# Two transformer layers on one core: a queue order rewritten by a search, with the transfer queue left as it was

## The chip, the core and the metric

The kernel runs on one core of a Trainium2 chip. The core has five instruction queues that run side by side: TensorE (PE, the matrix multiplies; PEld is its weight load), VectorE (DVE), ScalarE (ACT), GpSimd (POOL) and SyncE (SP, which here issues transfers only). Each queue starts its instructions in the order in which they stand in it, and waits for other queues through semaphores. The metric is the device time of one execution in microseconds (us), lower is better; for the kernel before, the median of three runs is 456.8 us.

## What is computed

One attention layer and one MLP layer, applied twice with the same weights, over 2048 tokens of width 512, in bfloat16:

```python
x = A_x
x = x + _A_ref(_layernorm(x), A_wqkv, A_wo)                  # 32 heads of 16, causal, window of 256
x = x + _B_ref(_layernorm(x), B_w1, B_b1, B_w2, B_b2)        # 512 -> 1792, gelu (tanh form), -> 512
x = x + _A_ref(_layernorm(x), A_wqkv, A_wo)
x = x + _B_ref(_layernorm(x), B_w1, B_b1, B_w2, B_b2)

# inside _A_ref
scores = einsum("bhqd,bhkd->bhqk", q, k) * 16 ** -0.5
scores = where(0 <= i - j < 256, scores, -1e9)
p = softmax(scores);  o = einsum("bhqk,bhkd->bhqd", p, v);  return o @ wo
```

B_x is not used.

## The kernel before

**The work.** The tokens are cut into 16 tiles of 128, and the two repetitions make 32 tiles in a row, tau 0 to 31; all weights stay in SBUF. Attention goes by blocks b of two tiles (16 blocks over both repetitions), the MLP by ten jobs J of two or four tiles. Each operation is a node of a plan with a key, and the texts name operations by these keys:

- Layer norm of tile pair b: `bsN`, `baN` (DVE statistics, lines 584 and 586), `vpN` (add epsilon, line 590, on POOL or DVE), `pwN` (the power -0.5, line 596, on POOL), `xnN` (DVE, line 606, subtract and scale). N is the tile in layer 0 (before attention) and 32 plus the tile in layer 1 (before the MLP). `txN` (SP, line 611) then transposes xn by a DMA into xnTA (layer 0) or xnTB (layer 1); for the first four and last two of them PE does it (`tpN`), and `teN` copies the result out.
- Projections of block b (PE, line 632): `qb_i`, `kb_i`, `vtau`. `qeb_i` and `vetau` copy them out of PSUM (on DVE, line 573, or ACT, line 575); `keb_i` (DVE, line 666) writes keys into KT with a parity mask. `vs` (SP, line 681) copies values to the other half of the partitions.
- Attention of block b, in up to ten visits g: `scb_g` (PE, line 733, scores into two pairs of PSUM banks), `exb_g_0` and `exb_g_1` (ACT, line 740, the exponential), `mkb_g_n` (line 761, multiplication with the 0/1 mask, on DVE or POOL). After half of the visits: `pvb_cp` (PE, line 783), `odb_cp` (DVE, line 792, transpose out of PSUM), `rcb_cp` (DVE, line 796), `nmb_cp` (line 800, DVE or POOL), `otb_cp` (DVE, line 806). Then `optau` (PE, line 632, output projection) and `rstau` (DVE, line 832, residual).
- MLP job J: `mJ_fc` (PE), then for the first six chunks `gbJ_fc` (DVE, line 855, bias) and `gaJ_f` (ACT, line 858, gelu), for the others `geJ_fc` (ACT, line 863, both). `xbtau` (POOL, line 871, x plus the second bias), `ytau` (PE), `yatau` (DVE, line 875, residual), and the store.

A suffix as in `op7.2` is the third part of a group of matmuls that can be queued apart. PSUM has eight banks; a group takes one, two or four of them and gives them back with the operation that reads it out, so a wait for a bank is a wait for an exponential, a copy or an `od`.

**What sets the order.** Building the plan numbers the nodes 0 to 3079 and says for each what it reads and writes. Three lists written out as numbers then decide everything else: `_ORDER` is a permutation of all nodes, from which each engine's queue takes its own nodes; `_ALT` names the nodes that run on their second engine (a copy on ACT instead of DVE, a mask or normalization on POOL instead of DVE, an epsilon on DVE instead of POOL); `_BANKS` gives the first PSUM bank of each group as it comes up. `_Plan.run` applies them:

```python
for i in _ALT:
    nodes[i]["eng"], nodes[i]["fn"] = nodes[i]["alts"][1]
...
for i in _ORDER:
    nd = nodes[i]
    assert nd["deps"] <= seen
```

`_Sched.op` then records each node on its engine in that order, works out from reads, writes and banks which counters of other engines it has to wait for, and lets each node add one to its own engine's counter (a transfer adds 16 to one of eight counters). So the n-th signal of an engine's counter in the trace is the n-th node of that engine's queue, and each node's end can be read from the trace by name.

Of the kernel before, what the change touches and what calls it, by code (L numbers as in the profile page):

```python
# [19 lines left out]
class _Sched:  # L20
# [147 lines left out]
    14, 17, 0, 22, 33, 4, 7, 34, 18, 37, 1, 19, 13, 36, 26, 3, 46, 15, 8, 27, 9, 35, 56, 16, 41, 20, 39, 57, 60, 28,  # L168
    58, 40, 61, 30, 38, 59, 24, 2, 64, 62, 106, 65, 63, 104, 21, 66, 10, 47, 49, 32, 67, 11, 25, 107, 105, 68, 108, 23,
    109, 69, 31, 54, 29, 5, 80, 70, 110, 81, 113, 71, 55, 111, 114, 112, 72, 115, 82, 42, 73, 6, 83, 150, 74, 116, 117,  # L170
    84, 126, 118, 127, 119, 128, 120, 129, 324, 194, 130, 85, 196, 97, 98, 99, 86, 195, 100, 48, 152, 366, 87, 101,
    368, 88, 75, 153, 90, 322, 103, 91, 76, 367, 151, 102, 77, 89, 78, 154, 12, 92, 79, 155, 198, 197, 131, 199, 93,
    156, 132, 94, 133, 157, 134, 200, 136, 135, 202, 137, 203, 138, 96, 139, 325, 323, 121, 158, 95, 326, 122, 204,
    140, 216, 327, 159, 201, 143, 217, 144, 205, 145, 146, 141, 519, 123, 218, 124, 328, 207, 147, 125, 329, 219, 212,
    208, 170, 213, 171, 172, 43, 330, 214, 370, 206, 173, 209, 148, 371, 174, 175, 210, 149, 160, 161, 162, 372, 331,
    176, 520, 163, 215, 177, 521, 374, 164, 373, 220, 44, 211, 376, 142, 165, 221, 178, 375, 45, 166, 167, 168, 180,
    522, 169, 222, 379, 223, 181, 380, 182, 230, 523, 224, 183, 524, 231, 381, 225, 179, 226, 369, 232, 233, 184, 227,
    384, 234, 378, 185, 228, 385, 332, 229, 333, 51, 383, 342, 187, 386, 52, 334, 235, 377, 343, 335, 50, 237, 344,
    337, 394, 388, 345, 396, 382, 338, 188, 238, 236, 387, 189, 239, 190, 395, 346, 339, 240, 389, 336, 191, 398, 243,
    641, 347, 400, 348, 349, 241, 340, 350, 390, 399, 242, 352, 359, 527, 244, 402, 391, 341, 392, 351, 353, 192, 403,  # L180
    354, 306, 355, 360, 356, 361, 404, 407, 639, 357, 362, 409, 363, 193, 248, 405, 249, 262, 528, 250, 263, 408, 412,
    264, 401, 252, 393, 253, 414, 245, 246, 254, 290, 255, 247, 256, 413, 427, 257, 563, 525, 410, 259, 565, 526, 260,
    278, 261, 279, 275, 564, 640, 416, 276, 411, 428, 53, 415, 272, 422, 287, 186, 397, 281, 282, 284, 365, 288, 285,
    277, 273, 423, 406, 280, 539, 289, 540, 566, 529, 251, 530, 541, 274, 531, 542, 283, 532, 543, 307, 265, 266, 267,
    258, 269, 270, 286, 308, 533, 309, 268, 310, 311, 271, 291, 312, 313, 417, 292, 418, 293, 314, 294, 315, 419, 567,
    642, 420, 295, 643, 568, 316, 317, 318, 421, 644, 319, 569, 320, 429, 647, 430, 321, 296, 648, 570, 571, 431, 297,
    573, 298, 299, 645, 424, 425, 434, 572, 646, 300, 576, 426, 301, 577, 302, 574, 303, 358, 304, 432, 544, 545, 578,
    305, 581, 546, 435, 433, 547, 583, 534, 436, 548, 535, 580, 549, 550, 582, 437, 536, 551, 552, 579, 537, 553, 591,
    538, 556, 592, 649, 584, 650, 557, 438, 558, 585, 593, 651, 439, 595, 575, 440, 559, 898, 596, 652, 594, 586, 441,
    560, 597, 653, 487, 654, 587, 599, 659, 598, 600, 660, 655, 588, 656, 661, 896, 601, 662, 604, 899, 589, 657, 605,  # L190
    456, 602, 658, 457, 442, 458, 443, 606, 452, 444, 445, 446, 663, 453, 609, 459, 610, 460, 454, 466, 603, 467, 608,
    449, 611, 897, 450, 447, 900, 478, 607, 451, 479, 469, 461, 470, 472, 590, 463, 503, 473, 664, 612, 481, 624, 471,
    482, 901, 468, 464, 665, 613, 462, 484, 485, 474, 666, 625, 480, 904, 475, 448, 902, 667, 905, 476, 483, 614, 486,
    465, 364, 477, 488, 455, 554, 615, 619, 620, 489, 903, 490, 491, 616, 683, 617, 492, 685, 493, 494, 495, 618, 496,
    684, 497, 561, 668, 498, 626, 627, 687, 628, 621, 688, 622, 499, 623, 500, 501, 689, 504, 631, 691, 505, 502, 692,
    506, 690, 507, 629, 508, 509, 693, 916, 632, 630, 696, 1018, 686, 510, 917, 697, 1019, 511, 1016, 918, 695, 512,
    694, 919, 698, 701, 513, 514, 703, 700, 676, 920, 515, 669, 516, 702, 670, 671, 517, 699, 906, 518, 711, 677, 704,
    712, 672, 678, 705, 679, 907, 673, 713, 706, 680, 675, 715, 707, 908, 716, 909, 717, 708, 719, 1017, 910, 709, 721,
    724, 1020, 710, 1021, 725, 633, 739, 1024, 718, 720, 740, 744, 726, 745, 722, 723, 729, 634, 911, 730, 912, 714,
    921, 731, 922, 727, 923, 732, 940, 913, 942, 733, 924, 728, 1022, 914, 941, 925, 1023, 734, 943, 915, 637, 635,  # L200
    1025, 944, 735, 945, 636, 736, 946, 948, 737, 562, 949, 738, 926, 746, 950, 741, 742, 555, 952, 743, 953, 674, 947,
    747, 955, 638, 748, 927, 928, 954, 832, 749, 958, 681, 751, 929, 682, 959, 750, 752, 933, 753, 754, 934, 960, 1036,
    757, 935, 951, 758, 1026, 961, 936, 755, 957, 937, 1037, 962, 756, 1027, 930, 956, 968, 1275, 1038, 969, 1039, 931,
    1028, 1040, 1029, 932, 963, 970, 1030, 971, 972, 964, 775, 973, 776, 777, 778, 781, 974, 779, 782, 976, 965, 783,
    978, 764, 1273, 966, 784, 785, 977, 981, 975, 765, 766, 982, 786, 979, 787, 788, 767, 983, 789, 768, 986, 987, 790,
    985, 770, 771, 1276, 772, 1274, 984, 980, 988, 773, 1060, 774, 1061, 989, 1064, 990, 1065, 991, 1066, 759, 1062,
    992, 760, 792, 761, 793, 762, 817, 993, 1068, 763, 797, 1070, 818, 1063, 794, 1277, 802, 967, 819, 1278, 1069, 798,
    795, 994, 827, 848, 799, 803, 807, 995, 804, 812, 805, 1071, 828, 808, 1067, 806, 829, 800, 1001, 791, 809, 813,
    820, 1002, 796, 830, 996, 1003, 831, 822, 814, 769, 1004, 997, 1005, 810, 998, 823, 821, 1072, 849, 850, 780, 824,
    833, 815, 834, 825, 801, 835, 836, 811, 851, 837, 838, 826, 852, 839, 816, 999, 853, 1000, 840, 841, 842, 843,  # L210
    1006, 1073, 1279, 844, 845, 1074, 1008, 854, 1280, 846, 855, 847, 856, 1075, 857, 1078, 880, 858, 1079, 859, 860,
    861, 862, 1080, 1031, 863, 1041, 1032, 1033, 1077, 1034, 1082, 1088, 1035, 1009, 865, 1081, 866, 1090, 1042, 1076,
    1043, 1007, 1281, 1044, 1395, 1089, 1083, 1282, 1045, 1091, 1092, 867, 1084, 1093, 881, 882, 864, 868, 869, 1094,
    883, 1085, 1096, 1086, 884, 1097, 870, 885, 871, 872, 1010, 873, 1098, 1011, 1101, 886, 874, 1102, 887, 1099, 1100,
    888, 875, 889, 1095, 1103, 876, 1393, 1106, 1087, 877, 1107, 878, 890, 1105, 891, 1104, 892, 1108, 879, 893, 1317,
    1014, 894, 1318, 1015, 1110, 1293, 1294, 1396, 1283, 1109, 1284, 1319, 1295, 895, 1285, 1286, 1296, 1287, 1321,
    1320, 1297, 1111, 1322, 1012, 1323, 1298, 1013, 1112, 1288, 1299, 1300, 1325, 939, 1301, 1113, 1326, 1046, 1302,
    1289, 1114, 938, 1047, 1290, 1327, 1291, 1048, 1049, 1394, 1324, 1115, 1121, 1050, 1122, 1330, 1292, 1123, 1328,
    1332, 1124, 1116, 1125, 1117, 1118, 1331, 1119, 1335, 1120, 1310, 1336, 1128, 1333, 1053, 1054, 1311, 1126, 1337,
    1345, 1129, 1127, 1055, 1334, 1056, 1130, 1346, 1312, 1131, 1313, 1329, 1057, 1132, 1349, 1347, 1134, 1133, 1339,  # L220
    1351, 1314, 1348, 1303, 1304, 1305, 1338, 1135, 1350, 1306, 1353, 1397, 1652, 1355, 1316, 1352, 1340, 1307, 1052,
    1354, 1398, 1308, 1358, 1341, 1315, 1356, 1360, 1163, 1164, 1147, 1165, 1401, 1166, 1359, 1363, 1167, 1148, 1309,
    1149, 1364, 1150, 1362, 1141, 1058, 1151, 1142, 1143, 1361, 1365, 1144, 1402, 1145, 1437, 1158, 1438, 1357, 1159,
    1342, 1160, 1399, 1161, 1367, 1439, 1400, 1441, 1366, 1152, 1343, 1153, 1443, 1440, 1368, 1051, 1344, 1442, 1059,
# [722 lines left out]
```

## Time and profile before

| | |
|---|---|
| three runs | 456.17, 456.8, 457.9 us; median 456.8 |
| profiled execution | 457.15 us, of which 455.3 us is the span from the first to the last instruction of the program; mean granted PE clock 0.996 |
| busy (share of the span) | PE 420.6 us (92%), ACT 385.0 (85%), DVE 352.7 (77%), PEld 230.2 (51%), POOL 193.4 (42%) |
| exponential, 128x1024 | 300 on ACT, 1041 ns each, 283.1 us in all |
| mask | 139 on DVE, 529 ns mean; 97 on POOL, 1089 ns mean |
| transfers | 47900 packets, 22.17 MB; 60 packets of 16384 bytes on queue 8, kind "instruction" |

Everything that is asked of a profile here is asked of that one execution, on its own clock, which starts at the first instruction. An instruction's duration as the trace shows it overlaps the next one's on DVE and ACT by about 0.1 us; where a text speaks of a service time, it is the time from the later of its start and the previous operation's signal to its own signal (512-wide mask: 0.335 us on DVE, 1.117 on POOL). PE's busy share counts overlapping, modelled matmul ends, so it says that PE is seldom without work, and not that it works at its peak; PE's losses are better seen from the distance between the signals of neighbouring operations.

### The profile page before, as it was taken

Reading aid. Unit: us, or ns where it says so; the run is one execution under the profiler, and the core shown is the slowest. Engines: PE = TensorE matmul, PEld = TensorE weight load, DVE = VectorE, ACT = ScalarE, POOL = GpSimd, SP = SyncE. Lnnn points to the kernel's source line nnn. Section 1 sums busy time; section 2 is a strip of 40 time slices with the busy share of each in tenths; the row PEclk is TensorE's granted clock in tenths of the full one; section 3 lists DMA queues with packets and bytes.
Section 4 is the critical chain, followed back from the end, with each engine's and each line's share of the span. In section 5 each row is a group of like instructions: output and inputs, shape, how many; then the busy total and the mean of one; then the engine's idle time right before and its main releaser. Section 6 shows DMA issues by size and latency. Waiting matters only on the chain.

```text
span 455.3 us, 16821 instructions
## 1 busy us (share of the span) xinstructions
PE 420.6 (92%) x7506; PEld 230.2 (51%) x7579; DVE 352.7 (77%) x655; ACT 385.0 (85%) x456; POOL 193.4 (42%) x217
## 2 busy tenths in 40 slices
PE   8998999985779997899999999999999999999997
PEld 4564646543344553445455454555554454444673
DVE  5999689886775778894799867977897598756862
ACT  2997968987889899789998998999888989899633
POOL 4164634237331247632472754274243443526130
PEclk9999999999899999999999999999999999999999
DMA  8695311201400211310012021010232003002110
GB/s 243 186 218 166 77 33 24 44 10 18 86 15 1 25 23 41 76 26 1 14 35 58 1 56 37 10 42 3 62 50 62 1 4 79 14 1 67 60 48 24
DMA packets 47972, 23.25 MB, mean 51 GB/s; under 512 B 33180, under 2 KB 47900, under 8 KB 47900
## 3 DMA queue, kind: packets, MB, share of 16 engines
q1 hardware_dynamic: 47900, 22.17, 21.0%
q8 instruction: 60, 0.98, 0.9%
q14 instruction: 12, 0.10, 0.1%
HBM read 8.00 MB, written 2.10 MB: 22 GB/s over the span
## 4 chain that ended last, share of the span: by engine, by line
PE 69%; DVE 15%; ACT 12%; issue 3%; DMA 2%; POOL 0%; SPq 0%
PE ps L632 52%; ACT E L740 11%; PE ps L733 8%; PE ps L783 7%; DVE KT L666 2%; DVE E L761 2%; DVE OD L792 2%; DVE xn L606 2%; PE ps L525 1%; DVE stat L584 1%; DMA xnTB<-xn 1%; DVE OT L806 1%; DVE X L832 1%; DMA xnTA<-xn 1%; DVE X L875 1%
## 5 line engine op out<-in xcount | busy, mean ns | idle before, releaser
L740 ACT ACTIVATE E<-ps 128x1024 bf16<-128x1024 f32 x300 | 283.1, 1041 | 42.4 <-PE ps L733 41.7
L761 POOL TENSOR_TENSOR E<-E,mask 128x512 bf16<-128x512 bf16 (+2 forms) x97 | 104.2, 1089 | 88.1 <-ACT E L740 88.0
L632 PE MATMUL ps<-xnTB,W_sb 128*128 128x512 bf16 (+1 forms) x542 | 110.2, 335 | 4.2 <-issue 1.6
L632 PE MATMUL ps<-W_sb,gT 128*128 128x512 bf16 x415 | 110.1, 380 | 3.3 <-issue 2.2
L761 DVE TENSOR_TENSOR E<-E,mask 128x512 bf16<-128x512 bf16 (+2 forms) x139 | 70.1, 529 | 10.3 <-ACT E L740 10.1
L632 PE MATMUL ps<-xnTA,Wqkv_sb 128*128 128x256 bf16 x512 | 74.6, 273 | 2.1 <-ACT E L740 0.7
L632 PEld LDWEIGHTS ps<-xnTB,W_sb 128*128 128x128 bf16 x560 | 50.6, 97 | 44.7 <-issue 4.1
L733 PE MATMUL ps<-QT,KT 32*128 32x128 bf16 (+3 forms) x1920 | 60.4, 232 | 10.9 <-ACT E L740 2.9
L632 PEld LDWEIGHTS ps<-W_sb,gT 128*128 128x128 bf16 x448 | 39.6, 98 | 43.2 <-issue 3.6
L733 PEld LDWEIGHTS ps<-QT,KT 32*128 32x128 bf16 x1920 | 28.6, 93 | 62.5 <-ACT E L740 36.9
L632 PEld LDWEIGHTS ps<-xnTA,Wqkv_sb 128*128 128x128 bf16 x512 | 46.9, 98 | 25.3 <-issue 3.9
L792 DVE STREAM_TRANSPOSE OD<-ps 128x1024 f32<-128x1024 f32 x32 | 39.8, 1244 | 21.5 <-PE ps L783 21.2
L863 ACT ACTIVATE gT<-ps,b1T 128x512 bf16<-128x512 f32 (+1 forms) x80 | 43.6, 609 | 10.3 <-PE ps L632 9.9
L871 POOL TENSOR_TENSOR Xb<-X,b2all 128x512 f32<-128x512 bf16 x32 | 38.5, 1209 | 24.8 <-DVE X L875 24.8
L783 PE MATMUL ps<-E,Va 64*17 64x128 bf16 (+3 forms) x1920 | 44.0, 230 | 4.1 <-ACT E L740 1.8
L666 DVE TENSOR_TENSOR KT<-ps,parmask 128x1024 bf16<-128x1024 f32 x32 | 38.8, 1212 | 11.1 <-PE ps L632 10.8
L783 PE MATMUL ps<-E,Vs 64*17 64x128 bf16 (+3 forms) x1920 | 44.6, 230 | 0.0
L783 PEld LDWEIGHTS ps<-E,Va 64*17 64x17 bf16 x1920 | 37.4, 84 | 13.9 <-issue 8.8
L584 DVE BATCH_NORM_STATS2 stat<-X 128x6 f32<-128x512 bf16 x64 | 42.7, 677 | 1.8 <-DMA X<-in_A_x_dram 1.7
L855 DVE TENSOR_SCALAR gT<-ps,b1T 128x512 bf16<-128x512 f32 (+1 forms) x60 | 36.5, 629 | 7.0 <-PE ps L632 6.4
L800 POOL TENSOR_TENSOR Nb<-OD,Rc 128x512 bf16<-128x512 f32 x19 | 20.2, 1061 | 49.9 <-DVE Rc L796 39.6
L632 PE MATMUL ps<-Wo_sb,OT 128*128 128x512 bf16 x120 | 37.2, 388 | 3.4 <-DVE OT L806 2.5
(50 smaller groups left out, 363.0 us busy)
## 6 DMA issues: line engine op xcount, KB each, us to landing
Vs<-Va SPq DMA_DIRECT2D x64, 68.0 KB, 2.1
W_sb<-in_B_w_dram SPq DMA_DIRECT2D x4, 512.0 KB, 5.5
out_dram<-X SPq DMA_DIRECT2D x16, 128.0 KB, 1.9
X<-in_A_x_dram SPq DMA_DIRECT2D x3, 512.0 KB, 7.3
Wqkv_sb<-in_A_wqkv_dram SPq DMA_DIRECT2D x4, 256.0 KB, 5.3
W_sb<-in_B_w_dram SPq DMA_DIRECT2D x1, 768.0 KB, 6.5
W_sb<-in_B_w_dram SPq DMA_DIRECT2D x2, 384.0 KB, 4.8
Wqkv_sb<-in_A_wqkv_dram SPq DMA_DIRECT2D x1, 512.0 KB, 7.1
```

The lines of the kernel that those rows point to most:

```text
L584: add("dve", lambda e, B, t=t, k6=k6: e.bn_stats(stat6[:, k6, :], X[:, t, :]), reads=["X%d" % t], writes=["st%d" % k6], key="bs%d" % (k + j))
L632: r = e.matmul(ps[:, B[g][0], cols], lhsT, rhs, start=st, stop=sp)
L666: add("dve", lambda e, B, g=g, i=i: e.tensor_tensor(out=KT[:, kb, 2 * i : 2 * i + 2].rearrange("p c m a q -> p a (c m) q"), in0=ps[:, B[g] ...
L733: x = e.matmul(ps[:, bk[r], o : o + n], KT[rows, kb, c, m].rearrange("p a q -> p (a q)"), QT[rows, c, q : q + n], start=True, stop=True)
L740: add("act", lambda e, B, g_=g_, gi=gi: e.activation(E[:, 2 * gi : 2 * gi + 2, e0 : e0 + 512], ps[:, B[g_][0] : B[g_][0] + 2, :], AF.Exp, ...
L761: fn = lambda e, B: e.tensor_tensor(out=Ew, in0=Ew, in1=Mw, op=ALU.mult)
L783: x = e.matmul(ps[32 * r : 32 * r + VW, B[g][par], c % 2 * 2 * P + lo : c % 2 * 2 * P + hi], V[rows, (2 * b + m // 2) % VR, c * HC + 2 * r ...
L792: add("dve", lambda e, B: e.transpose(OD[:, s].rearrange("p a c q -> p (a c q)"), ps[:, B[g][0] : B[g][0] + 2, :]), reads=["ps:" + g], wri ...
L800: return e.tensor_tensor(out=Nb[:, s, :].rearrange("p (k a d) -> p a k d", a=2, d=Dh), in0=sums[:, :, :, 0:Dh], in1=rc[:, :, :, None].to_b ...
L855: add("dve", lambda e, B, g=g, fc=fc: e.tensor_scalar(out=gT[:, fc, c0 : c0 + M], in0=ps[:, B[g][0], 0:M], scalar1=b1T[:, fc : fc + 1], sc ...
L863: add("act", lambda e, B, g=g, fc=fc: e.activation(gT[:, fc, c0 : c0 + M], ps[:, B[g][0], 0:M], AF.Gelu_apprx_tanh, bias=b1T[:, fc : fc + ...
L871: add("pool", lambda e, B, t=t, xs=xs: e.tensor_tensor(out=Xb[:, xs, :], in0=X[:, t, :], in1=b2all[:], op=ALU.add), reads=["X%d" % t, "b2a ...
```

## The change

All three lists are rewritten; nothing else is. What a program that reads both versions by name finds:

- SP's queue: all 159 transfers in the same order. PE: the same 1615 operations, 580 of them at another place, 17 places away at most.
- 82 nodes run on another engine: masks 32 from DVE to POOL and 28 from POOL to DVE; `nm` 4 to POOL and 2 to DVE; `vp` 2 to POOL and 4 to DVE; copies out of PSUM 6 from DVE to ACT and 4 from ACT to DVE. DVE then has 649 operations (655 before), ACT 440 (438), POOL 217 (213).
- 32 of the 639 PSUM groups lie in another bank.

The diff of the three lists is some 350 lines of numbers. Its second list in full up to the last lines, for the look of it:

```diff
 _ALT = [
-    60, 66, 74, 79, 108, 112, 120, 125, 164, 169, 184, 210, 219, 336, 369, 373, 377, 378, 383, 392, 397, 401, 405, 406,
-    410, 411, 523, 553, 566, 570, 580, 594, 598, 602, 607, 686, 690, 695, 709, 714, 718, 723, 727, 753, 930, 937, 943,
...
+    60, 66, 74, 79, 108, 120, 125, 164, 169, 184, 191, 210, 219, 336, 369, 373, 377, 378, 382, 383, 392, 405, 415, 523,
+    553, 566, 574, 579, 589, 594, 598, 602, 603, 608, 633, 643, 653, 686, 694, 695, 709, 714, 722, 723, 915, 930, 937,
...
```

What it does to the queues at the places that the prediction speaks of, with the numbers put back into names (-: before, +: after):

```diff
 start
-ACT  te0 te2 qe0_0 qe1_0 ex0_0_1
+ACT  te0 qe0_0 qe1_0 ex0_0_1
-DVE  te1 i5 xn2 xn3 te3 i6 bs4 ke0_0 bs7 ke1_0 b1c bs5 ve1
+DVE  te1 xn3 xn2 i6 te3 te2 bs4 b1c ke0_0 ba4 bs7 ke1_0 bs5 bs6 ba5 ve1
 34 to 49 us
-DVE  rs0 bs32 bs33 mk1_4_1 mk1_3_0 ba33 ba32 mk1_4_0 ke3_0 ve5 xn33 bs11 xn32 od1_0 xn9 rc1_0 qe3_1 ke3_1 ve6 ... gb0_3 xn8 gb0_4
+DVE  xn8 rs0 bs32 bs33 ba32 mk1_4_1 mk1_4_0 ba33 ke3_0 bs11 od1_0 xn33 xn32 rc1_0 bs10 ke3_1 qe3_1 xn9 mk1_6_0 ve6 ... gb0_4
 68 to 71 us
-DVE  ke4_1 mk2_3_0 qe4_1 mk2_4_0 xn34 mk2_4_1 mk2_2_1 xn35
+DVE  ke4_1 mk2_3_1 qe4_1 xn34 mk2_4_0 mk2_4_1 xn35 mk2_2_1
 102 to 116 us
-DVE  ot3_0 xn15 mk3_7_0 mk3_9_0 mk3_9_1 mk3_8_1 xn14 ke6_1 qe6_1 xn37 xn36 od3_1
+DVE  ot3_0 mk3_6_0 mk3_8_0 vp36 xn15 mk3_9_0 mk3_8_1 mk3_9_1 xn14 ke6_1 xn37 xn36 od3_1
-POOL pw14 vp36 mk3_6_0 mk3_7_1 pw36 mk3_5_0 mk3_8_0 mk4_0_0
+POOL pw14 mk3_7_0 mk3_5_0 pw36 mk3_7_1 mk4_0_0
-ACT  ex4_0_1 ex4_0_0 ex4_1_0
+ACT  ex4_0_1 ex4_0_0 qe6_1 ex4_1_0
 120 to 126 us
-DVE  ba39 vp38 xn39 mk4_2_0 mk4_4_0 xn38 mk4_3_1 mk4_4_1 mk4_3_0
+DVE  ba39 mk4_3_1 xn39 mk4_4_0 xn38 mk4_4_1 mk4_3_0
-POOL xb4 pw38 mk4_5_0 nm4_0 mk4_6_0
+POOL xb4 vp38 pw38 mk4_2_0 nm4_0 mk4_5_0 mk4_7_1 mk4_6_0
 173 to 191 us
-ACT  ex6_5_0 ve15 ex6_5_1
+ACT  ex6_5_0 ex6_5_1
-DVE  ba43 ba42 mk6_3_1
+DVE  ba42 ba43 mk6_2_1 ve15 mk6_3_1
 267 to 272 us
-DVE  od9_1 rc9_1 xn25 ya12 ot9_1 ya13 mk10_2_0 xn49 rs18 ba26 xn48 rs19 mk10_4_0
+DVE  od9_1 rc9_1 nm9_1 ya12 ot9_1 ya13 xn49 rs18 xn48 rs19 ba26 mk10_4_1
 364 to 372 us
-DVE  ya20 bs57 rs24 rc13_0 ba57 bs56 ba56 ke15_0 xn57 mk13_7_1 mk13_6_0 ot13_0 mk13_8_0 ke15_1
+DVE  ya20 rc13_0 rs24 ba57 bs56 ba56 ot13_0 ke15_0 mk13_7_1 xn57 ke15_1 mk13_6_0
-POOL vp56 pw56 nm13_0 mk13_8_1
+POOL nm13_0 vp56 xb23 pw56 mk13_8_0 mk13_7_0
```

## The prediction, made before the changed kernel's times were known

> **What bounds the kernel now.** I read the page first, for the engines and the clock:
>
> ```profile
> PE 420.6 (92%) x7506; PEld 230.2 (51%) x7579; DVE 352.7 (77%) x655; ACT 385.0 (85%) x456; POOL 193.4 (42%) x217
> ...
> PEclk9999999999899999999999999999999999999999
> ...
> PE 69%; DVE 15%; ACT 12%; issue 3%; DMA 2%; POOL 0%; SPq 0%
> ```
>
> TensorE (PE) is the bound: busy for 92%, and 69% of the chain that ended last. POOL is nowhere on that chain by name. One slice has a lower granted clock. Next comes the chain in order of time (start, length, what):
>
> ```profile
> 47.62 1.26 DVE xn L606
> 48.95 3.09 DMA xnTA<-xn
> ...
> 69.60 0.67 DVE E L761 x2
> 70.86 4.35 DMA xnTB<-xn
> ...
> 100.35 7.45 ACT E L740 x8
> 107.83 2.19 DVE E L761 x3
> 110.34 1.13 DVE KT L666
> 112.71 1.17 DVE OD L792
> 114.29 0.70 DVE Nb L800
> 115.02 0.72 DVE OT L806
> 115.79 1.44 PE ps L632 x3
> ...
> 173.18 4.69 ACT E L740 x5
> 178.36 2.76 ACT E L740 x3
> ```
>
> Most of its pieces are PE at work; these are the places where PE waits. Third, the stretches around the lower clock (PE, PEld, DVE, ACT, POOL busy us, granted clock, DMA):
>
> ```profile
> 112.00:116.00 4.00, 1.01 (x21) 0.56 (x23) 3.63 (x7) 3.43 (x4) 0.00 (x0) 0.98 0.65 82
> 116.00:120.00 4.00, 4.00 (x45) 1.34 (x44) 2.34 (x4) 2.58 (x4) 2.88 (x3) 0.59 0.39 85
> ```
>
> PE works 1.01 of 4 us, and then runs 4 us at 0.59. Last, I matched each engine's operations, in the order of its list, with the completion signals in the trace. A projection or MLP step of PE (2x256 or 1x512 columns) completes 0.216 us after the one before when nothing holds it. Measured against such undisturbed steps for each kind of operation, PE loses 45 us in all: 15.6 of them between 100 and 140 us, 7.3 between 160 and 200, and under 2 in each 20 us after 200. So from 200 us on there is little to win, and what is won before is kept.
>
> **The change part by part.** Nothing is computed that was not before. SP's list of 159 transfers is identical, so the loads, transposes and copies are issued in the same order. 82 operations change engine; by median service times (512-wide mask: DVE 0.335, POOL 1.117; copy from PSUM: DVE 0.60, ACT 0.49) POOL gets 6.9 us more, ACT 1.0 more, DVE 4.2 less. The table loads of ACT stay at 18, of 1283 ns each, so their number costs nothing either way. The rest are places in the queues: 580 of PE's 1615 operations move, by 17 places at most. For each moved operation I compared its new place with the end of its latest operand in this trace; where the slack stays positive I cost it at nothing, covered by the PE work put in front of it, and if that cover is gone it costs at most the 0.2 us of a step jumped over. What is left:
>
> (a) Start, 8 to 23 us. The evacuation te2 goes from ACT to DVE (0.435), and b1c moves up in front of ke0_0 (0.08). te3 gains 0.21, since PE transposes its tile first (tp3 ends at 9.75 instead of 9.97). So ke0_0, and with it the first scores, end some 0.3 us late; later copies and ke1_1 keep 0.14. I take +0.2, between 0 and +0.4.
>
> (b) 34 to 52 us. xn8 ended at 48.88 and its transfer, waiting in SP's queue for it, landed at 52.03, so PE began k4_0.0 0.58 us late. Now xn8 stands before rs0 (33.7 us), its factor pw8 being ready at 31.4. SP still issues tx9 ahead of tx8, and xn9 now ends near 43.0 instead of 40.8, before the 44.88 at which SP issued tx9. The wait goes: -0.6 (between -0.6 and 0, should the copies ahead on SP hold both). Next due is sc1_7's bank, which od1_0 now gives back 1 us earlier.
>
> (c) 68 to 75 us. xn35 comes some 0.4 us earlier (mk2_2_0 and mk2_3_0 have left DVE, and it passes mk2_2_1); m1_4.0 waited 0.48 for its transpose. -0.3 (-0.5 to 0).
>
> (d) 104 to 116 us, the largest. In the fence, DVE's three masks from 107.83 take 2.19; their medians are 0.47 + 0.47 + 0.20 = 1.14. The second one, mk3_9_1, took 1.42, and ended at 109.82 when POOL's mk3_8_0 (from 107.87) ended at 109.39. That mask is now on DVE ahead of them; mk3_7_0 goes to POOL instead, in front of mk3_5_0 and mk3_7_1. So the masks end 0.4 to 1.0 earlier. DVE also loses qe6_1, 0.60 us between ke6_1 and od3_1: ACT does it in the 2.34 us that it idled before 112.57. od3_1, OT and the output projection at 115.79 come 1.0 to 1.6 earlier. But mk3_8_0 in DVE's queue now holds back vp36, xn15 and mk3_9_0 if POOL holds it (up to 0.4). -1.0 (-1.6 to +0.2). The low clock may stay, since PE still has little to do there.
>
> (e) 120 to 126 us. pw38 on POOL is now followed by a mask that is ready (mk4_2_0, 1.1 us); before, POOL then waited for ACT. xn39 needs pw38, so it starts just after that mask has:
>
> ```profile
> L606 DVE TENSOR_SCALAR xn<-X,statmv,rstd x64: 314/406/1328, 4.7 to 437.9; 128x512 bf16<-128x512 bf16 x64
> ```
>
> Min, median and max: an xn takes 0.3 to 0.4 us, or up to 1.3. The long ones are those beside a POOL operation that has already begun: xn8, xn24, xn48, xn29, xn57 and xn60 took 0.88 to 1.25 by completion signals, and each ended within 0.22 us of the POOL operation's end. Behind xn39 stand the masks mk4_4_0, mk4_4_1 and mk4_3_0, for which PE's pv4_0 waits. Hold +1.0, less mk4_2_0 (0.33) and part of vp38: +0.5 (-0.5 to +0.8).
>
> (f) 173 to 191 us. ACT runs exponentials without a pause, and PE waits for their banks (v16.0 loses 1.17). ve15 (0.49) leaves ACT's queue in front of ex6_5_1, and DVE takes it in a slot with slack. -0.5 (-0.6 to 0).
>
> (g) 267 to 278 us. DVE is the chain. mk10_2_0 leaves it (0.34) and nm9_1 comes (0.70 instead of POOL's 1.07 between rc9_1 and ot9_1); but xn48, now free 0.4 earlier, still meets POOL's mk10_3_0. -0.2 (-0.8 to +0.2).
>
> (h) 365 to 373 us. ot13_0 now stands in front of ke15_0, and so ke15_0 waits for nm13_0 on POOL, which is put ahead of vp56 and done by 366. +0.1 (0 to +0.7).
>
> (i) Holds elsewhere. In this trace 29 of 203 masks and xn on DVE were held, 18.1 us over the medians. 32 masks come to POOL and 28 leave it, at 18.1/217 = 0.083 us per POOL operation: +0.3 us of DVE time, of which a fifth reaches the chain (DVE masks and xn are 2.2% + 1.6% of it, 17 of their 96 us busy). +0.1 (-0.5 to +3).
>
> [...]
>
> **Sum.** 0.2 - 0.6 - 0.3 - 1.0 + 0.5 - 0.5 - 0.2 + 0.1 + 0.1 = -1.7 us. The profiled execution took 457.15 us (span 455.3 and 1.85 around it), 0.35 above the median of 456.8 and inside the runs' 456.17 to 457.9. From it the sum gives 455.45; from the median, by which a result is judged, **455.1 us**.
>
> **Rivals.** First, nothing: gains of under 1 us are taken back at the next exponential or evacuation that comes on time. For it speaks that ACT is busy for 85%; against it, that PE's losses after 200 us are so small. 456.8.
>
> Second, slower: POOL's masks hold DVE. Of the 32 masks new on POOL, each could hold a DVE neighbour for its full 1.12 us, 36 us of DVE time, of which a fifth, 6 to 7 us, reaches the chain. The place is wherever POOL has a ready mask behind a pow or beside a pair of masks, as at 121 us. It decides once DVE's held time grows from 18 to some 40 us (22 x 0.18 = 4.0, which is the gain of 1.7 and the 2.3 of a slower result). For 45 us, a gain of 1.7 and a loss of 4.9: 460.0. Against it speaks that collisions go as well: behind pw42, pw56 and pw60 POOL's next operation was ready, and now it is not.
>
> Third, more: if (d) gives PE enough work before 116 us, the 4 us at 0.59 go too, which is 4 x 0.41 = 1.6 us. 453.5. [...]
>
> Fourth, the change doesn't do what it is said to do for landings and page fetches: with SP's list unchanged, and each pv at most 3 instructions from its old place in PE's program, no landing but those of (b) and (c) moves; they alone give 456.8 - 0.9 = 455.9.
>
> **How the numbers follow.** About 0.5% (2.3 us) is what a measurement of this kernel can tell from no change: faster is below 454.5, slower above 459.1. Chances: forecast 0.45, nothing 0.15, slower 0.20, more 0.13, fourth 0.07. Faster: a third of the forecast (0.15) and nearly all of the third rival (0.12), 0.27. Slower: 0.17 of the second rival, and 0.04 from the forecast's and the first rival's upper ends, 0.21. The same: 0.52. The range, 452.8 to 459.9, leaves out half of the second rival and the far ends of the third and the forecast. The forecast alone spans 453.5 to 457.
>
> **What would show it.** (b) k4_0.0 without a wait near 52 us; (c) the same for m1_4.0 at 75; (d) a chain with less than 2.19 us of masks at 107 and the output projection before 115; (e) xn39 over 0.9 us long; (f) v16.0 earlier; (i) the sum of held DVE masks and xn, 18.1 us before. The prediction fails if that sum grows past 30 us, if pv waits on POOL masks appear, or if a second stretch shows a lower clock.

## The result and the profile after

The changed kernel takes 458.98 us (median of 8 runs, 457.73 to 460.26) against 456.82 us (8 runs, 456.17 to 457.90): 1.0048 times the time before, 95% interval 1.0036 to 1.0061, so some 2.2 us slower. The forecast was 455.1. The profiled execution is one of the shortest of the eight: 457.73 us, span 455.8, only 0.58 above the profiled execution before. What the trace of it shows is thus a part of the loss; the rest has to be found in the scatter of the other runs (spans 455.8 to 458.5, where six of the kernel before's eight times lie between 456.4 and 457.1). Three executions in a slow state (granted clock 0.56 to 0.84; one each of the kernel before, b_only_d and a_sp2) are in no ratio below.

Three lines of the page after: busy time of PE, granted clock in 40 slices, and the engines' shares of the chain that ended last.

```profile
PE 420.9 (92%) x7506; PEld 229.8 (50%) x7579; DVE 353.8 (78%) x649; ACT 386.6 (85%) x458; POOL 200.9 (44%) x221
...
PEclk9999999999899999999999999999999999999999
...
PE 64%; ACT 19%; DVE 11%; DMA 2%; issue 2%; SPq 1%; POOL 0%; DVEq 0%
```

PE's share of the chain fell from 69 to 64%: it waits more. Where is told by the operations' ends, matched by name in both traces, wherever both queues of PE have done the same set of operations. The difference after minus before (negative: ahead) moves like this; smaller moves are left out:

| us | difference moves by | at |
|---|---|---|
| 19, 21 | +0.28, then back to +0.03 | start (a) |
| 42, 52 | -0.31, -0.50 | sc1_7, k4_0.0 (b) |
| 69 | **+1.12** | q5_0 |
| 75 | -0.38 | m1_4.0 (c) |
| 90 to 117 | -1.43 | pv3_1, sc4_1, op7.2 (d) |
| 118 to 126 | +0.80, then -0.40 | sc4_4 to q7_0.1, then pv4_0 and sc4_6 |
| 127 | **+2.08** | m2_3.0 |
| 180, 183 | -0.49, -0.17 | v16.0, pv6_0 (f) |
| 235, 241 | **+0.93, +0.94** | k10_1.0, k11_0.0 |
| 273 to 279 | -0.91 | sc10_5 to sc10_7 (g) |
| 365 to 391 | -0.07 | (h) |
| end | +0.51 in all | |

So the foreseen gains came, nearly all at their size, and four losses came that the sum did not have (in bold; +5.1 in all). The chain of the trace after shows (d) and the largest loss (start, length, what; line numbers are one higher than before):

```profile
107.82 1.62 DVE E L762 x3
...
110.90 0.96 DVE xn L607 x2
111.85 1.17 DVE OD L793
...
120.27 1.19 DVE xn L607
...
121.53 1.19 SPq L612
122.73 0.45 issue
...
123.25 4.18 DMA xnTB<-xn
127.43 0.27 issue
127.70 1.03 PE ps L633 x4
```

The masks of step (d) take 1.62 instead of 2.19, and the copy of 0.60 that stood behind them is gone. But then an xn takes 1.19 us, SP's next issue comes 0.45 late, the transpose tx38 takes 4.18 from its issue to its landing, and PE's m2_3.0 has waited for it. In the trace of before tx38 was issued at the same time, 123.29, and took 2.42; there m2_3.0 waited for a copy, and began a microsecond earlier:

```profile
125.74 0.61 DVE QT L573
126.35 0.35 issue
126.70 1.24 PE ps L632 x5
```

What made it slow is a packet of kind "instruction". The trace records each packet: 60 of 16384 bytes on queue 8, about one for every 250 of the 15,085 matmuls and weight loads that PE executes; they take 0.9 to 1.7 us each. By that count the text takes them for fetches of PE's program, and calls the place in a program where one ends and the next begins a border. Between 123 and 128 us after has one, and one of 8192 bytes on another queue:

```profile
q8 instruction: 1, 0.02, 1.6%
q14 instruction: 1, 0.01, 0.6%
```

The first is on its way from 125.11 to 126.40 us. A transpose lands in sixteen parts, each with a signal of its own; these signals are meant where a time is given for a transpose's packets. Fifteen of tx38's came from 125.53 to 125.62 and the last at 127.43, 1.03 after the fetch had ended: one part of sixteen was held. In before the fetch came at 125.55, level with tx38's packets (125.58 to 125.71), and did no harm. The same is seen in both traces: a transpose lands 1.22 us after its issue ends (within 0.2), and, tx7 apart, 1.9 to 3.3 us after it where a fetch of a program was begun ahead of its packets (tx10 in after: level with them) and was not over when its issue ended. After has 12 late transposes and before 11, tx7 among them; what matters is which.

The stretches around the low clock (PE, PEld, DVE, ACT, POOL busy us, granted clock, DMA), and the row of all xn (min, median, max in ns):

```profile
112.00:116.00 4.00, 1.58 (x23) 0.73 (x28) 3.20 (x5) 3.35 (x4) 0.10 (x1) 1.00 0.44 90
116.00:120.00 4.00, 3.95 (x47) 2.00 (x41) 2.54 (x7) 3.55 (x4) 3.54 (x5) 0.57 0.45 97
```

```profile
L607 DVE TENSOR_SCALAR xn<-X,statmv,rstd x64: 370/406/1515, 4.7 to 438.4; 128x512 bf16<-128x512 bf16 x64
```

PE has 1.58 us of work in the first 4 us instead of 1.01, and the clock of 116 to 120 us is as low all the same (0.57, before 0.59). The median xn is what it was, and the longest one is longer (1515 ns, before 1328).

### The profile page after: what moved, and what is told of

It is laid out like the page before. It is cut to its first block, busy times and chain, and to the rows that moved or that the text cites. A ratio compares the mean times of both kernels' runs of the same rounds, so it can differ in the third digit from the quotient of the medians.

```text
span 455.8 us, 16822 instructions
## 1 busy us (share of the span) xinstructions
PE 420.9 (92%) x7506; PEld 229.8 (50%) x7579; DVE 353.8 (78%) x649; ACT 386.6 (85%) x458; POOL 200.9 (44%) x221
## 4 chain that ended last, share of the span: by engine, by line
PE 64%; ACT 19%; DVE 11%; DMA 2%; issue 2%; SPq 1%; POOL 0%; DVEq 0%
PE ps L633 47%; ACT E L741 14%; PE ps L734 7%; PE ps L784 7%; ACT gT L864 2%; DVE OD L793 2%; PE ps L526 1%; DMA xnTB<-xn 1%; ACT gT L859 1%; DVE xn L607 1%; DVE E L762 1%; DVE OT L807 1%; DVE X L833 1%; DVE stat L585 1%; DMA xnTA<-xn 1%
## 5 line engine op out<-in xcount | busy, mean ns | idle before, releaser
L762 POOL TENSOR_TENSOR E<-E,mask 128x512 bf16<-128x512 bf16 (+2 forms) x101 | 111.5, 1117 | 117.8 <-ACT E L741 117.8
L762 DVE TENSOR_TENSOR E<-E,mask 128x768 bf16<-128x768 bf16 (+2 forms) x135 | 67.7, 523 | 9.1 <-ACT E L741 8.7
L801 POOL TENSOR_TENSOR Nb<-OD,Rc 128x512 bf16<-128x512 f32 x21 | 22.4, 1066 | 45.0 <-DVE Rc L797 37.1
```

The source lines that it names most:

```text
L762: fn = lambda e, B: e.tensor_tensor(out=Ew, in0=Ew, in1=Mw, op=ALU.mult)
L801: return e.tensor_tensor(out=Nb[:, s, :].rearrange("p (k a d) -> p a k d", a=2, d=Dh), in0=sums[:, :, :, 0:Dh], in1=rc[:, :, :, None].to_b ...
```

## The experiments

**Theory 1:** the gains came, and the losses sit at four places: at 69 and 127 us a transpose meets a fetch of PE's program, at 235 and 241 us an xn on DVE is held by a POOL operation. **Theory 2** (the prediction's second rival): the masks added on POOL hold DVE all along. **Theory 3:** more stretches of low clock in most executions than in the profiled one.

### Four repairs of the changed kernel

a_warm14 (four dummy matmuls fewer at the start, so that by that count every border of PE's program comes 8 instructions, a matmul and a weight load for each of the four, later in the work):

```diff
+_SKIP = {21, 23, 25, 31}  # warm6 warm8 warm10 warm16
+_ORDER = [_n for _n in _ORDER if _n not in _SKIP]
...
```

> The changed kernel with four of the 18 dummy matmuls at the start of PE's queue left out (they warm PE up, nothing reads them). Every queue keeps its order; every page border of PE's program comes 8 instructions later. Theory 1 (the gains came, but they put two transposes, tx10 at 69 us and tx38 at 127 us, into a fetch of PE's program): the 16 KB fetches at 66.9 and 125.1 us start some 0.2 us later or more, behind the last packets of tx10 and tx38; q5_0 ends 1.1 us and m2_3.0 2 us earlier, 2 to 3 us in all, so about 456.5 us. Theory 2 (the masks that came to POOL hold DVE all along): no change, 458 to 459.5. Theory 3 (more stretches of low clock in most executions): no change in the best execution, 457.5 to 459.

a_tx10 (xn11 and xn10 in each other's place; here and for a_dve the numbers are put back into names):

```diff
-DVE  ot1_1 xn10 ya1 rs3 bs35 mk2_1_0 xn11
+DVE  ot1_1 xn11 ya1 rs3 bs35 mk2_1_0 xn10
```

> The changed kernel with xn11 and xn10 in each other's place on DVE, as they stood before the change. Theory 1: tx11 goes out 2.5 us earlier, so tx10 goes out right when xn10 ends (63.2 us) and has landed by 65.8, ahead of the fetch at 66.9; q5_0 no longer waits, -1.1 us at 69 us. The rest, tx38 included, moves along with PE, so some -0.8 in all, 458.1. Theory 2 and theory 3: the landing at 68.9 is a symptom that the next exponential takes back, 458.8.

a_dve (xn44 and xn47 put back):

```diff
-DVE  mk8_1_0 od7_1 ... bs46 xn44 od8_1 ... rs17 xn47 rs16 ve20 mk9_4_0
+DVE  mk8_1_0 xn44 od7_1 ... bs46 od8_1 ... rs17 rs16 ve20 xn47 mk9_4_0
```

> The changed kernel with xn44 put back ahead of od7_1 (in the changed kernel it stands just ahead of od8_1 and lasts 1.24 us beside POOL's xb13) and xn47 put back behind rs16 and ve20 (1.31 us beside POOL's mk9_1_0). Theory 1: k10_1 at 235 us and k11_0 at 241 us each lose 0.9 us to these two holds; both go, some -1.7 us, 457.3. Theory 2: other masks and xn are held in their place, since POOL's list is unchanged: -0.3, 458.7. Theory 3: 458.5 to 459.

a_all (the three edits together):

> The changed kernel with all three repairs together: four dummy matmuls fewer, xn11 ahead of xn10, xn44 and xn47 in their old places. Theory 1: -1.1, -2 and -1.7, less what a later exponential takes back, so 454.5 to 455.5 us, under the kernel before (456.8). Theory 2: 458. Theory 3: the time of the best execution falls, but the runs scatter over 2.5 us as those of the changed kernel do, with clocks of 0.989 to 0.996.

Measured, against 456.77 (medians; ratio to before with its interval): a_warm14 459.31, 1.0043 (1.0024 to 1.0063); a_tx10 458.82, 1.0042 (1.0021 to 1.0062); a_dve 458.20, 1.0025 (1.0006 to 1.0043); a_all 458.39, 1.0032 (1.0006 to 1.0059). All four medians miss theory 1's numbers, while the traces show that most of the edits did locally what they were to do:

- tx10 lands clean in a_warm14, a_tx10 and a_all, and q5_0 gains 1.12 in each. But in a_warm14 and a_all the fetch that now came later made PE itself wait: pv2_0 at 72 us loses 1.22 and 1.24, with all its operands there for 1.3 us (in a_warm14 PE stops in the midst of it from 71.14 to 72.12; the fetch had landed at 70.68).
- In a_dve k10_1 gains 0.87 and k11_0 0.94; pv9_0 at 248 us, which waits for a DVE mask, gives 0.94 back. The second hold, in the chain of after (xn47, then rs16, whose bank PE waits for):

```profile
241.03 1.31 DVE xn L607
242.34 0.61 DVE X L833
...
243.08 1.47 PE ps L633 x10
```

- tx38 lands late in all four. The fetch moved with PE's own waiting, not by 8 instructions.
- In all four, and in after, xn39 ends 0.14 to 0.15 us after POOL's mk4_2_0. That is step (e)'s hold, which I had taken to be absent because xn39 ended earlier than before (121.45 against 121.89). Its factor pw38 came 1.25 earlier, so with an xn of the usual length it would have ended at 120.6.

The profiled execution of a_dve, a span of 458.8 us, shows what a long run consists of: the granted clock is low at 43.9, at 105.4 and from 115.6 to 122.4 us (mean 0.985), and from 33 to 45 us it loses 2.0, half of it to the clock and the other half because sc1_7 waited for a fetch that was begun 1.05 us later than in after. So theory 3 has a part in this execution at least. Theory 2 is not supported: by the measure of the prediction, 35 of 199 masks and xn of DVE are held in after, 19.8 us, against 29 of 203 and 18.1 us.

### Steps (d) and (e) alone

Both versions of the list have done the same set of operations at many places, and hold the same PSUM banks there, so a stretch of one can be put into the other.

```diff
 a_no_e    after:  places 801 to 895 (120 to 134 us, step e) as before
 a_fix     after:  the same, places 1489 to 1806 (224 to 269 us) as before, xn11 ahead of xn10
 b_only_d  before: places 716 to 800 (99 to 120 us, step d) as after
 b_only_e  before: places 801 to 895 as after
```

> The changed kernel with the 95 places of the list from 120 to 134 us (step e) put back as they were: vp38 and mk4_2_0 on DVE again, the mask behind xn39. Theory 1 (a POOL mask holds xn39, so tx38 goes out 0.9 us late and meets a fetch of PE's program): xn39 ends at 120.6 instead of 121.45, tx38 has landed by 124.5 to 125, ahead of the fetch at 125.1, and m2_3.0 ends 1.8 to 2 us earlier. PE then has no pause of 2.5 us at 125 to 127.7, so the runs also lose the second or third stretch of low clock that follows it: 456.5 to 457, with the scatter of the kernel before. Theory 2 (POOL's added masks hold DVE all along): only one of 32 goes, -0.3, 458.6. Theory 3 (low clock in the stretch of 102 to 119 us, which is left as it is): 458 to 458.5, and the runs scatter as widely as before.

> The changed kernel with three stretches put back: 120 to 134 us, 224 to 269 us (where xn44 and xn47 are held), and xn11 ahead of xn10 at 60 us. Theory 1: -2 at 127 us, -1.1 at 69, -1.8 at 235 and 241, less some 0.9 that a later DVE mask takes back at 248: 455 us, under the kernel before. Theory 2: 457.5. Theory 3: single executions at 454.5, but a median of 457 with runs up to 460.

> The kernel before with nothing but the stretch from 99 to 120 us of the change (step d: qe6_1 on ACT, mk3_8_0 on DVE, mk3_7_0 on POOL). Theory 1: pv3_1 -0.5, the output projection at 117 us -1.0 to -1.4, and as xn38, tx38 and the fetch all move along, m2_3.0 keeps -1.0; so 455.8 to 456.2. A rival within theory 1 (PE being a microsecond ahead is enough to bring the fetch onto tx38): m2_3.0 +1.5, 457.5 to 458. Theory 2: masks that came to POOL hold DVE, no gain, 456.8. Theory 3: the low clock at 116 us stays and now falls on work, 457 with more scatter.

> The kernel before with nothing but the stretch from 120 to 134 us of the change (step e). Theory 1: xn39 ends right behind mk4_2_0, near 122; pv4_0 comes 0.3 to 0.5 earlier as DVE has two operations less ahead of it, and with it the fetch, from 125.55 to 125.1 or 125.2, ahead of tx38's packets at 125.58: tx38 lands 1.7 us late and m2_3.0 ends 1.2 to 1.7 us later; a pause of 2 us there brings another stretch of low clock in part of the runs: 458 to 458.8. The sum of the prediction (+0.5): 457.3. Theory 2: 457. Theory 3: 456.8.

Measured, against 456.95: a_no_e 458.52, 1.0040 (1.0021 to 1.0059); a_fix 456.26, 0.9994 (0.9977 to 1.0010); **b_only_d 456.21, 0.9980 (0.9971 to 0.9990)**; **b_only_e 458.79, 1.0051 (1.0033 to 1.0068)**.

Step (d) alone is a gain and step (e) alone is a loss as large as that of the whole change. The chain of b_only_d shows (d) as the sum had it:

```profile
107.52 1.62 DVE E L777 x3
...
111.56 1.17 DVE OD L808
...
114.63 0.82 PE ps L648 x3
```

The output projection starts at 114.63 instead of 115.79. The difference to before goes from -0.39 to -1.78 at 117 us, and since tx38 and the fetch move along (first packets at 123.77, fetch at 123.85), it stays -1.72 to the end. In b_only_e xn39 ends 0.15 after mk4_2_0, pv4_0 gains 0.46, the fetch comes at 125.22 ahead of tx38's packets (125.47), tx38 lands at 127.24, and m2_3.0 loses 1.51.

The hold of (e) is seen where the two engines' rows of after are laid side by side (timeline around 120 us: start, length, engine, line, operation; the bracket says how long the engine was idle before, and for what):

```profile
120.27 1.17 DVE L607 TENSOR_SCALAR xn<-X,statmv,rstd 128x512 bf16<-128x512 bf16 x1 [1.02 <-POOL rstd L597]
```

```profile
120.14 1.15 POOL L762 TENSOR_TENSOR E<-E,mask 128x512 bf16<-128x512 bf16 x1
```

Before, with no POOL operation beside it, it was

```profile
121.47 0.41 DVE L606 TENSOR_SCALAR xn<-X,statmv,rstd 128x512 bf16<-128x512 bf16 x1 [0.81 <-POOL rstd L596]
```

The mask began 0.13 us before the xn, and the xn ended when the mask had: 1.17 instead of the median 0.41. In six traces (after, the four repairs and b_only_e) xn39 ended 0.14 to 0.15 us after the mask.

a_no_e and a_fix, which missed theory 1's numbers (456.5 to 457, and 455), refute its first form: with (e) put back, tx38 was late all the same. In their traces SP, whose list of transfers is the same, issues one of the two transposes 0.5 us late, as it does in after. Here are SP's two issues (timeline: start, and the length of the pair) before,

```profile
121.99 2.50 SPq L611 DMA_TRANSPOSE xnTB<-xn  x2
```

and after:

```profile
121.53 2.95 SPq L612 DMA_TRANSPOSE xnTB<-xn  x2
```

The order of a queue is not its program. In SP's rows of the trace each further wait of an operation is an instruction of its own: 15 of them stand ahead of tx39 before and 13 after, since the change took three away there and added one: tx8 no longer waits for xn8, because the transfer ahead of it waits for xn9, which now stands behind xn8 on DVE (tx5 and tx10 likewise; vs7_1 got one). With 13 instead of 15 such instructions ahead, the pause of 0.5 us, which in before would fall in the time that SP waits for xn39 anyway, falls between tx39 and tx38. In a_fix and a_tx10, where tx10 has its own wait again (14), it falls between xn39's end and tx39: one instruction further, as a border of SP's own program would. The packets of 8192 bytes on queue 14 move in the same way: with 13 such instructions (after, a_no_e, a_dve, a_warm14) one begins 0.55 to 0.57 us after tx38's issue does, and in the twelve other traces it begins 0.36 us or more ahead of that issue. Whose program they hold the trace doesn't say, so that the pause is a border of SP's is argued; that it moves with the number of waits is shown.

### SP's and PE's programs

```diff
 a_no_e_sp: a_no_e, two more waits ahead of vs11_0; a_fix_sp: a_fix, one
+            if nd["key"] == "vs11_0":
+                for _ in range(2):   # a_fix_sp: range(1)
+                    S_.prog["sp"].append(lambda e, s=S_.cnt_sem["dve"]: e.wait_ge(s, 1))
```

```diff
 b_cdfg: before, places 498 to 544, 716 to 800, 1144 to 1260 and 1807 to 1905 as after
```

```diff
 b_pe16: before, with warm2 and warm3 in five pieces
+        def warm(e, bk, cuts):
+            for lo, hi in zip(cuts, cuts[1:]):
+                ins = e.matmul(ps[:, bk, lo:hi], gT[:, 0, 0:P], gT[:, 0, lo:hi], start=True, stop=True)
...
+            cuts = (0, 128, 256, 384, 448, 512) if h in (2, 3) else (0, 512)
```

> a_no_e plus two waits on SP that are long met, ahead of vs11_0, where SP has time. The change took three waits from SP's program before tx39 and added one (an earlier xn on DVE is then covered by the wait of the transfer ahead); with 196 instead of 198 wait slots SP's issue of tx38 comes 0.52 us after that of tx39, in after and a_no_e alike, and 0.11 in the kernel before. Theory 1, refined (a border of SP's own program, moved by two instructions, delays tx38 by 0.5 us, and so it loses a race against the fetch of PE's program): with two instructions more the gap is 0.1 again, tx38's packets start ahead of the fetch, m2_3.0 does not wait; 1.7 us less, and no pause at 125 us that brings low clock: 456.5 to 457, runs within 1.5 us. Rival (the gap is tx39's own or the fetch comes first in any case): as a_no_e, 458.5.

> a_fix plus one such wait (it has 197 slots, since tx10 has its own wait again). Theory 1, refined: tx39 follows xn39 by 0.1 us instead of 0.49, tx38 wins the race, m2_3.0 1.7 us earlier: 454.5 to 455 us, and the upper runs of a_fix (455.7 to 456.9 of span) go. Rival: 456.3, as a_fix.

> The kernel before with four stretches of the change: c (69 to 75 us), d (99 to 120), f (173 to 179) and g (269 to 284). SP's program keeps its 198 slots. Theory 1: b_only_d's 456.2, less 0.3 to 0.4 (c), 0.5 (f) and 0.9 (g): 454.5 to 455, runs close together. Theory 2 (POOL's added masks): 456. Against theory 1 would be a loss at 127 us: c and d together bring PE 1.8 to 2.2 us ahead there.

> The kernel before, with two of the dummy matmuls at the start of PE's queue cut into five pieces each (the same columns, 16 instructions more); nothing else. Theory 1: every border of PE's program comes 16 instructions earlier, so the fetch at 125.55 us starts 0.2 to 0.4 us earlier, ahead of tx38's packets at 125.58; tx38 lands 1.7 us later and m2_3.0 ends 1.1 to 1.7 us later: 458 to 458.8, with a wide scatter. If the fetch follows a wait of PE rather than its place in the program: no change, 456.8.

Measured, against 457.12: a_no_e_sp 458.40, 1.0018 (0.9999 to 1.0036); **a_fix_sp 454.35, 0.9924 (0.9895 to 0.9954)**; **b_cdfg 454.66, 0.9943 (0.9924 to 0.9962)**; b_pe16 462.86, 1.0108 (1.0085 to 1.0132).

a_fix_sp differs from a_fix by one wait that is long met. tx39 follows xn39 without a pause, tx38 lands at 124.64, and m2_3.0 no longer waits for it: the medians go from 456.26 to 454.35, the ratios from 0.9994 to 0.9924. b_cdfg takes only steps of the change whose gains the prediction had priced, and nothing of (b), (e) and (h): it is 2.5 us faster than before (by the ratio 2.6).

a_no_e_sp missed, since the two equal waits came out as one instruction (14 in its trace). Its chain has the pause one place earlier than after has it, ahead of tx39, and tx38 late again:

```profile
119.97 0.45 issue
120.42 1.33 SPq L628
...
121.86 4.30 DMA xnTB<-xn
```

b_pe16 missed by its size and by its mechanism, and showed the most. tx38 was not hit (packets at 126.51, fetch at 126.56: both had moved by 1). But 16 more instructions that cost nothing themselves (at 38.2 us PE is 0.7 ahead of before) made the kernel some 5 us slower (5.7 by the medians, 4.9 by the ratio). Its chain, around 397 us, says why ("issue" is time in which PE waited for nothing that the profile shows):

```profile
398.61 0.33 PE ps L742 x8
398.94 1.57 issue
400.50 2.55 PE ps L641 x11
```

Before, the same three pieces were

```profile
396.78 0.33 PE ps L733 x8
397.11 0.16 issue
397.27 2.85 PE ps L632 x12
```

A fetch was on its way from 397.94 to 399.07. The same is seen at 38.38 (2.44 us, fetch 38.45 to 39.58) and 311.24 (1.12, fetch 309.76 to 310.96): PE stops in the midst of ready work and goes on 1.2 to 1.4 us after the fetch has landed. Of the three stops 1.6, 0.9 and 1.3 us stay against the trace of before (at 38 us the kernel before waited for a bank in any case), which is most of what the profiled execution loses; at the end it is 3.7 behind. Its granted clock is lower too (0.989 against 0.996), and what the median loses beyond 3.7 no trace shows.

### Both causes of the lost race

```diff
 a_sp2: after; a_no_e_sp2: a_no_e; in both one wait more ahead of vs11_0 and one ahead of vs11_1
+            if nd["key"] in ('vs11_0', 'vs11_1'):
+                S_.prog["sp"].append(lambda e, s=S_.cnt_sem["dve"]: e.wait_ge(s, 1))
```

> The changed kernel as it is, with one wait that is long met ahead of vs11_0 and one ahead of vs11_1 on SP, where SP has time: SP's program then has as many instructions ahead of tx39 as in the kernel before. Theory 1, refined (two causes lose tx38's race: SP's program border, 0.5 us, and stretch e, which brings the fetch of PE's program 0.4 us forward): tx38 goes out 0.1 us after tx39 instead of 0.52, its packets start near 125.0, level with the fetch at 125.1; won in part of the executions, so 457 to 458.5. If SP's border alone decides: 456.8, runs close together. If it doesn't matter: 458.8.

> The changed kernel with stretch e put back and with those two waits, so that both causes of the lost race are gone. (The two equal waits of a_no_e_sp at one place came out as a single instruction: its trace shows 14 wait instructions of SP's own before tx39, a_no_e 13, the kernel before 15.) Theory 1, refined: tx39 0.1 us behind xn39, tx38 0.1 behind tx39, landed ahead of the fetch; m2_3.0 1.7 us earlier than in a_no_e and without a pause before it: 456.5 to 457, and nearly all runs below 456 of span. If the race is lost for another reason: 458.4, as a_no_e and a_no_e_sp.

Measured, against 456.70: a_sp2 459.15, 1.0052 (1.0031 to 1.0073); **a_no_e_sp2 456.48, 0.9990 (0.9976 to 1.0003)**.

a_sp2 came out above the 457 to 458.5 that were expected of it: SP's pause is gone (tx38 0.11 after tx39), but xn39 is held (it ends 0.15 after mk4_2_0), and the fetch at 125.86 is ahead of the packets at 126.24. In a_no_e_sp2 both are gone, tx38 lands at 124.25, and m2_3.0 waits for the copy ahead of it as it did before:

```profile
124.28 0.61 DVE QT L590
124.89 0.35 issue
125.24 1.24 PE ps L649 x5
```

m2_3.0 gains 1.91 against after and pv4_0 0.55 before it. Either cause alone is enough to lose the race of tx38's packets against the fetch; with both removed the whole loss of 2.2 us is gone, though 69, 235 and 241 us are as in after.

The sixteen traces agree on what decides it. In the ten in which tx38 is late, the fetch begins between 0.02 us ahead of the end of its issue and 0.85 behind it; in the six in which it lands 1.22 after its issue, the fetch begins 1.06 to 1.85 behind.

The scatter goes too: the 12 spans of a_no_e_sp2 are 453.9 to 455.9, 11 of a_sp2 455.5 to 460.6. The likely link is the pause. PE does little but pv4_0 from 122.3 to 127.7 us when tx38 is late, and a stretch of low clock behind it falls on MLP work that nothing hides. After's profiled execution has none there (1.00 from 128 to 132 us); here is one that has, a_no_e's with a span of 459.1 us (PE, PEld, DVE, ACT, POOL busy us, granted clock, DMA):

```profile
124.00:128.00 4.00, 2.28 (x140) 1.57 (x137) 4.00 (x6) 2.82 (x4) 1.16 (x1) 1.00 0.38 78
128.00:132.00 4.00, 3.00 (x18) 1.16 (x20) 1.58 (x4) 0.78 (x2) 0.39 (x1) 0.57 0.08 17
```

The granted clock of all executions supports the link and doesn't prove it. Its mean is 0.990 over the 104 of the nine variants that have tx38 late in their trace, 0.993 over the 35 of the four that don't (b_pe16, with its stops, left out), and 0.992 over 106 of the kernel before. But over the changed kernel's own eight it is 0.993, so in these there is no more low clock than before; if it makes them slow, then by where it falls.

The low stretches are 3.41 us long (or twice that) and lie on a grid of that step in each trace. Which idle stretch of PE is followed by one I could not settle, since two at 102 us with PE busy for 46 and 47% (after, before) were followed by full clock, and two at 40 us with 49 and 54% (a_dve, a_no_e) were not.

## Why the prediction was wrong, point by point

- **(a), (b), (c), (f), (h) came near to what was worked out:** +0.03 by 21 us, -0.8, -0.38, -0.49 (with pv6_0 -0.66), -0.07, for +0.2, -0.6, -0.3, -0.5, +0.1; (b), (f) and (h) end up to 0.2 past their lower bounds. **(d)** was -1.43 for -1.0, inside its bounds, and alone makes the kernel 0.7 us faster. **(g)** was -0.91 for -0.2, just past its lower end of -0.8: sc10_5 to sc10_7 each gained. The four priced gains (c), (d), (f), (g) by themselves were forecast at -2.0 and measured at -2.5 (b_cdfg).
- **(e) is the step that failed.** It was put at "+0.5 (-0.5 to +0.8)". The hold was there near the size named (+1.0), xn39 0.86 over its median, and the path that the step followed came out too: pv4_0, which waits for the masks, loses 0.4 there against a_no_e_sp2. What the step did not follow is the transfer behind it: it went on to the masks, and left out tx39 and tx38. Measured: m2_3.0 +2.08 in after, +1.51 with (e) alone, and the kernel with (e) alone +1.8 us.
- **The fourth rival's "no landing but those of (b) and (c) moves" is false, and the method had it built in.** I compared places with the ends of operands, and took a landing to be its issue plus a constant. In the traces of before and after a landing is, tx7 apart, 1.22 or 1.9 to 3.3 us after the end of the issue, by which of the two comes first, its packets or a fetch; so tx38's came 1.7 us later though neither its xn nor its issue did. For tx10, whose landing is the +1.12 at 69 us, the issue moved as well: the change puts xn11 behind xn10 on DVE while SP issues tx11 first, so tx10 went out at 64.56 instead of 63.27 and then met a fetch. The trace of before had it to read: 11 late transposes, fetches beside all but tx7, and tx38 with no margin (fetch at 125.55, packets at 125.58). The prediction relied on SP's list being unchanged; SP's program was not, by two instructions.
- **(i)** put the added held time at 0.3 us beside (e)'s hold, and a fifth of it on the chain: +0.1. Held time grew by 1.7 in all (18.1 to 19.8), and the places were wrong. "A fifth reaches the chain" is an average; xn44 and xn47, held for 0.93 and 0.98 us, stand right ahead of od8_1 and rs16, whose banks PE waits for, and all of it reached the chain: +1.87, inside the bounds (up to +3).
- **The second rival** came near the time (460.0) by luck: it needed 40 us of held time. **The third** expected the 4 us at 0.59 to go with more work for PE ahead of them; PE had 1.58 us of it instead of 1.01, and they ran at 0.57. That the clock follows from how long PE is idle was an estimate, and the stretches at 102 and 40 us leave it open; the change made a new pause (at 125 us) and did not remove the old one.

The account closes with three ratios, each times 456.8 us. The change costs +2.2 (1.6 to 2.8). Without the lost race, a_no_e_sp2: -0.5 (-1.1 to +0.1). Without the losses at 69, 235 and 241 us as well, a_fix_sp: -3.5 (-4.8 to -2.1; six runs, -2.8 by the medians), where the traces have 1.1 and 1.9 for those. What it leaves is the forecast's gains without (e): -2.2 by the forecast. Both a_fix_sp and b_cdfg beat both kernels.

Open are why a fetch is begun up to 1 us later in some executions (sc1_7 in a_dve), why tx7 lands 2.7 to 5 us after its issue in every trace, in two with no fetch beside it (before, a_fix_sp), and which part of a long run is due to such fetches and which to the clock.

## What to carry to other kernels

A change of order alone changed three things here that the order doesn't show: how many wait instructions SP's program has, where in the work a border of a program falls, and which transfers meet a fetch. So list for each transfer the distance of its packets from the nearest instruction packet, and don't count on a small margin; the largest loss here sat behind a margin of none, and one idle wait instruction in the right queue was worth 1.9 us. Follow a held operation through everything that it feeds, transfers first. Where the profiled execution is shorter than the median, look for a new pause, and in other executions for the clock behind it (0.57 from 128 to 132 us in a_no_e's trace, 1.00 in after's).

## What the runs showed of the hardware

- **Fetches of PE's program, by the count above, cost time in two ways.** Where one is under way between the end of a DMA transpose's issue and its packets, the transpose lands 2.1 to 3.3 us after that end instead of 1.22 (before, after). PE stops for 1.0 to 2.4 us in the midst of ready work and goes on 1.2 to 1.4 us after a fetch has landed (a_warm14, b_pe16). Moving the borders by 16 instructions cost some 5 us of 457 (b_pe16).
- **SP pauses for 0.5 us between two transfers**, at a place that moves with the number of its wait instructions (after, a_fix, a_no_e_sp); with one more wait that is long met no pause was left there (a_fix_sp).
- **Two identical waits ahead of one operation left one instruction**, by the wait instructions that SP's rows show (14 where 15 were meant), and its pause stood one place earlier accordingly.
